# Attention and early expert products in 64-row tiles of the TensorE array

## The chip, the cores and the metric

One core of a Trainium2 chip (trn2). The metric is the device time of one execution in microseconds (us), lower is better. The span of a profile is from the first to the last instruction, about 1.8 us less than the time of the same execution. The profiled execution for the kernel before was a separate one of 525.9 us, some 7 us longer than the timed ones (517.5 to 520.2), so losses read from its trace are a few microseconds too large. Four batches of experiments ran on four chips, and the kernel before took 517.3, 523.5, 524.3 and 524.6 us on them (medians). So kernels of different batches are compared by their ratio to the kernel before of the same batch, and never by microseconds of the clock alone.

## The reference

Attention over 8 batches of 8 heads, with 576 pooled queries (the mean of two neighbours), 1152 keys and head size 64; its output is a matrix of 4608 rows of 512. Then each row goes through the two-layer network of its expert (8 experts, 512 to 1024 to 512), given by `domain_id`.

```python
q_pool = q.reshape(B, H, S // 2, 2, D).mean(axis=3)
scores = q_pool @ k.transpose(0, 1, 3, 2) / sqrt(D)
attn = softmax(scores)
x = (attn @ v).transpose(0, 2, 1, 3).reshape(B * S // 2, H * D)
for e in range(8):
    mask = domain_id == e
    out[mask] = maximum(x[mask] @ w1[e], 0) @ w2[e]
```

## The kernel before

The unit of work is a pair of heads; there are 32. A pair is cut into 12 steps, so there are 384 steps. A step makes 432 columns of scores for each of the two heads on TensorE, in the transposed form (128 keys on the partitions), and one exp instruction on ScalarE over 128 x 864. A pair needs nine "AV" chunks of 128 keys: ten products each, with the exp tile as weights and 65 columns of v (64 and a column of ones, which gives the sum of the softmax).

The head size is 64, and a product spans up to 128 rows of the array (`128*128` in the timeline). The two heads of a pair lie on rows 0 to 63 and 64 to 127, and q is kept in two copies, `qz`, with zeros in the other head's half. The scores of one head are thus a product over all 128 rows, half of them zero.

```python
def score(t):                               # one step
    p, s_ = divmod(t, SPP)                  # SPP = 12
    s = spsum.tile([P, 2, 512], FP32, name="s")
    ...
    for r in range(2):                      # the two heads
        nc.tensor.matmul(
            s[:, r, o : o + n], lhsT=kq[p][:, c * P : (c + 1) * P],
            rhs=qz[p % 2][r][:, q0 : q0 + n], start=True, stop=True)

def av(p, c):                               # one chunk of 128 keys
    for h in range(2):
        for i in range(NQ):                 # NQ = 5
            nc.tensor.matmul(
                acc[p][h][:, i * (D + 1) : (i + 1) * (D + 1)],
                lhsT=e_[:, h, o + QO[i] : o + QO[i] + P],
                rhs=v16[p % NV][:, c, h, 0 : D + 1],
                start=c == 0 and i == 0, stop=c == NC - 1, skip_group_check=True)

AVS = {3: 0, 4: 1, 5: 2, 7: 3, 8: 4, 9: 5, 11: 6, 12: 7, 13: 8}   # step: chunk
```

k and q of the next pair are transposed on TensorE against the identity (`burst_k`, `burst_q`), all in 128-row products, or 96-row ones for q (`QP = 96`). The finished rows are scattered to `x_slot` in HBM, sorted by expert; before that, `x_slot` is filled with a pattern (`init_x`, four transfers) and some rows of padding are scattered. From step 220 on, eight tiles of 128 rows of the expert work are done between the attention steps ("early tiles"); 32 tiles remain for a tail after the last exp.

The softmax here doesn't subtract the row's maximum and nothing guards it: scores larger than these inputs give would overflow.

## Time and profile before

The kernel before took 517.7 us (median of 3; with a fourth run, beside the changed kernel, 518.7 us, 517.5 to 520.2).

| what | value | where it is read |
|---|---|---|
| exp instructions, distance where nothing waits | 0.783 us | timeline of ScalarE |
| first and last exp start | 11.7 and 372.3 us | timeline of ScalarE |
| 383 x 0.783 us | 299.9 us | |
| loss of the exp chain | 372.3 - 11.7 - 299.9 = 60.7 us | worked out |
| after the last exp starts | 524.1 - 372.3 = 151.8 us | 32 expert tiles, 3.84 us each, and the ending |

ScalarE's chain of exps sets the pace up to 372 us (it is busy 78.9 of the 80 us from 140 to 220 us), TensorE sets it after that (busy 99.8 of the 100 us from 400 to 500 us). "Loss" in this document is always the time by which a stretch of exps is longer than 0.783 us each.

The first parts of the page of the kernel before: span, busy time by engine, then 40 slices of the span with the busy share in tenths, the granted TensorE clock and the busy share of the DMA engines.

```profile
span 524.1 us, 12917 instructions
...
PE 453.3 (86%) x5536; PEld 321.4 (61%) x5536; DVE 234.3 (45%) x561; ACT 348.1 (66%) x455; POOL 172.2 (33%) x294
...
PE   6679890599999999969999899999679999999990
...
ACT  2579890499999999949999899999412323323220
...
PEclk9698996699999999979999999999989999999997
...
q8 instruction: 45, 0.74, 0.6%
...
L439 ACT ACTIVATE e<-s 128x864 f16<-128x864 f32 x384 | 308.4, 895 | 59.7 <-PE s L427 56.5
```

ACT and PE are both near 9 in the attention, with a hole in the seventh and eighth slices (80 to 98 us). The last line says that ScalarE spent 59.7 us idle before exps and that almost all of it ended with a score product. The line `q8` is an instruction queue: 45 packets, 0.74 MB.

Two stretches of the timeline of the kernel before, at 98 us and from 152 us (start, duration, engine, line, operation, count, and in brackets the idle time ahead and what ended it).

```profile
98.10 0.89 ACT L439 ACTIVATE e<-s 128x864 f16<-128x864 f32 x1 [18.08 <-PE s L427]
...
152.62 0.53 PE L427 MATMUL s<-qz,kq 128*128 128x144 f16 x4
...
152.99 0.47 PE L450 MATMUL acc<-v,e 128*128 128x65 f16 x10
...
153.40 0.53 PE L427 MATMUL s<-qz,kq 128*128 128x288 f16 x4
...
153.77 0.61 PE L391 MATMUL tp<-ident,kp 128*128 128x128 f16 x8
...
154.22 0.53 PE L427 MATMUL s<-qz,kq 128*128 128x432 f16 x2
```

Durations of matmuls overlap (the scores of 152.62 last to 153.15, and AV starts at 152.99), so starts are what counts: 0.37 us from a step's scores to its AV chunk, ten AV products 29 to 35 ns apart, eight transposes 55 to 56 ns apart. The first line is the hole: one exp waits 18.08 us at step 67. There the fills of `x_slot` and the padding scatters wait for each other, and a load of q comes late behind them.

### The profile page before, as it was taken

The numbers are of one execution on the slowest core, as the hardware profiler recorded it, in microseconds if no ns is written. First come the engines' busy times: TensorE is split into PE (matmuls) and PEld (weight loads), VectorE is DVE, ScalarE is ACT, GpSimd is POOL, SyncE is SP. The second block draws the span as 40 slices with busy tenths as digits, with TensorE's granted clock in tenths as the row PEclk, the third lists the DMA queues.
The fourth block names the chain that finished last, engine by engine and source line by source line (L and its number), as shares of the span: only waits on it lengthen the run. The fifth ranks groups of instructions, "written<-read, shape, count | busy, mean of one in ns | idle before, by whom it ended". The sixth has DMA issues, their size and how long they took to land.

```text
span 524.1 us, 12917 instructions
## 1 busy us (share of the span) xinstructions
PE 453.3 (86%) x5536; PEld 321.4 (61%) x5536; DVE 234.3 (45%) x561; ACT 348.1 (66%) x455; POOL 172.2 (33%) x294
## 2 busy tenths in 40 slices
PE   6679890599999999969999899999679999999990
PEld 4457670477777777758778778777545555555540
DVE  3378640255355455525656466544323332332220
ACT  2579890499999999949999899999412323323220
POOL 5100211663613414410741633410221554312421
PEclk9698996699999999979999999999989999999997
DMA  8991547999997994994799799910051599922211
GB/s 215 240 201 22 126 135 165 250 209 236 227 231 166 192 187 72 198 216 93 171 205 208 164 153 199 203 41 34 21 176 41 125 232 269 248 93 76 86 54 44
DMA packets 53620, 81.55 MB, mean 156 GB/s; under 512 B 4783, under 2 KB 39343, under 8 KB 53553
## 3 DMA queue, kind: packets, MB, share of 16 engines
q0 software_dynamic: 35312, 50.60, 50.1%
q1 hardware_dynamic: 18032, 29.44, 21.1%
q8 instruction: 45, 0.74, 0.6%
q10 hardware_dynamic: 208, 0.59, 0.4%
q14 instruction: 23, 0.18, 0.1%
HBM read 95.48 MB, written 21.54 MB: 223 GB/s over the span
## 4 chain that ended last, share of the span: by engine, by line
PE 31%; issue 23%; DMA 18%; ACT 14%; POOL 9%; DVE 2%; POOLq 0%; SPq 0%; ACTq 0%
PE s L427 16%; ACT e L439 14%; PE acc L450 8%; POOL out_dram L349 5%; DMA x_slot<-pat 3%; DMA out_dram<-osb,xs 3%; DMA k<-in_k_dram 3%; DMA w2h<-in_moe_w_dram 2%; DMA x_slot<-pat,padr 2%; POOL x_slot L349 2%; PE m L535 2%; DMA xs<-x_slot 2%; DMA q<-in_q_dram 2%; PE m L547 2%; PE tp L391 1%
## 5 line engine op out<-in xcount | busy, mean ns | idle before, releaser
L439 ACT ACTIVATE e<-s 128x864 f16<-128x864 f32 x384 | 308.4, 895 | 59.7 <-PE s L427 56.5
L427 PE MATMUL s<-qz,kq 128*128 128x432 f16 (+2 forms) x1152 | 208.3, 290 | 12.1 <-ACT e L439 7.1
L450 PEld LDWEIGHTS <-e 128*128 128x128 f16 x2880 | 129.3, 98 | 43.4 <-issue 3.5
L450 PE MATMUL acc<-v,e 128*128 128x65 f16 x2880 | 139.1, 195 | 1.6 <-DVE xb L466 0.8
L427 PEld LDWEIGHTS <-kq 128*128 128x128 f16 x1152 | 100.2, 99 | 39.2 <-issue 18.5
L349 POOL DMA_INDIRECT out_dram<-osb,xs x40 | 40.2, 1006 | 124.4 <-ACT osb L701 65.4
L349 POOL DMA_INDIRECT x_slot<-xb,addr x40 | 42.9, 1071 | 94.3 <-issue 59.1
L678 PE MATMUL hp<-xt,w1h 128*128 128x384 f16 (+3 forms) x384 | 61.4, 311 | 1.8 <-DVE xt L664 0.9
L695 PE MATMUL op<-w2h,hT 128*128 128x512 f16 x256 | 59.8, 379 | 0.0
L678 PEld LDWEIGHTS <-w1h 128*128 128x128 f16 x384 | 34.1, 99 | 28.9 <-issue 4.6
L97 POOL DMA_DIRECT2D vs<-in_v_dram x32 | 24.2, 757 | 65.0 <-DVE v L374 52.9
L685 DVE TENSOR_SCALAR hT<-hp 128x384 f16<-128x384 f32 (+2 forms) x36 | 22.8, 632 | 49.1 <-PE hp L678 40.1
L701 ACT COPY osb<-op 128x512 f32<-128x512 f32 x20 | 11.7, 586 | 49.5 <-PE op L695 40.3
L683 ACT ACTIVATE hT<-hp 128x384 f16<-128x384 f32 (+2 forms) x36 | 19.8, 550 | 36.0 <-PE hp L678 35.6
L464 DVE RECIPROCAL rr<-acc 128x5 f32<-128x5 f32 x64 | 12.2, 190 | 70.4 <-PE acc L450 61.1
L365 DVE TENSOR_TENSOR qp<-q 96x768 f16<-96x768 f32 x32 | 30.3, 946 | 22.5 <-DMA q<-in_q_dram 22.4
L695 PEld LDWEIGHTS <-hT 128*128 128x128 f16 x256 | 24.1, 98 | 24.3
L466 DVE TENSOR_TENSOR xb<-acc,rr 128x320 f16<-128x320 f32 x64 | 31.5, 492 | 2.6
L404 PE MATMUL tp<-ident,qp 96*128 96x96 f16 x192 | 14.0, 210 | 18.1 <-DVE qp L365 18.1
L412 DVE COPY qz<-tp 64x576 f16<-64x576 f16 x64 | 28.8, 450 | 0.8
L383 DVE COPY kp<-k 128x576 f16<-128x576 f16 x62 | 25.0, 444 | 7.5 <-DMA k<-in_k_dram 7.5
L391 PE MATMUL tp<-ident,kp 128*128 128x128 f16 x256 | 20.0, 222 | 6.9 <-DVE kp L383 6.4
(93 smaller groups left out, 305.2 us busy)
## 6 DMA issues: line engine op xcount, KB each, us to landing
q<-in_q_dram SPq DMA_DIRECT2D x31, 576.0 KB, 10.1
vs<-in_v_dram POOLq DMA_DIRECT2D x32, 288.0 KB
k<-in_k_dram POOLq DMA_DIRECT2D x31, 288.0 KB
w1h<-in_moe_w_dram POOLq DMA_DIRECT2D x16, 512.0 KB
w2h<-in_moe_w_dram POOLq DMA_DIRECT2D x16, 512.0 KB
x_slot<-pat SPq DMA_DIRECT2D x4, 1285.0 KB, 9.3
xs<-x_slot SPq DMA_DIRECT2D x5, 385.5 KB, 4.6
xs<-x_slot SPq DMA_DIRECT2D x3, 642.5 KB
```

Source lines behind the costliest of these rows:

```text
L97: nc.gpsimd.dma_start(vs[:, :, :, :], v[b, h : h + 2].rearrange("h (p c) d -> p h c d", p=P))
L349: ins = nc.gpsimd.indirect_dma_start(out=dst[:, :], out_offset=bass.IndirectOffsetOnAxis(ap=ap, axis=0), in_=src, in_offset=None, **kw,)
L365: nc.vector.tensor_tensor(out=qp[:, :, :, :].rearrange("p j h d -> p h j d"), in0=q2[:, :, :, 0:D], in1=q2[:, :, :, D : 2 * D], op=ALU.add,)
L383: nc.vector.tensor_copy(kp[:, :, hh, :], loaded[p]["k16"][:, hh, :, :])
L391: nc.tensor.transpose(mt[:, c * P : (c + 1) * P], in_=kp[:, c, :, :].rearrange("p h d -> p (h d)"), identity=ident16[:, :],)
L412: nc.vector.tensor_copy(qz[p % 2][r][lo : lo + 64, :], mt[lo : lo + 64, P : P + Sp])
L427: nc.tensor.matmul(s[:, r, o : o + n], lhsT=kq[p][:, c * P : (c + 1) * P], rhs=qz[p % 2][r][:, q0 : q0 + n], start=True, stop=True,)
L439: nc.scalar.activation(e_[:, :, o : o + W], st.pop(t)[:, :, 0:W], AF.Exp, bias=0.0, scale=0.0625)
L450: nc.tensor.matmul(acc[p][h][:, i * (D + 1) : (i + 1) * (D + 1)], lhsT=e_[:, h, o + QO[i] : o + QO[i] + P], rhs=v16[p % NV][:, c, h, 0 : D ...
L466: nc.vector.tensor_tensor(out=xb[b][:, :, hh * D : (hh + 1) * D], in0=a[:, :, 0:D], in1=rr[:, :].unsqueeze(2).broadcast_to([P, NQ, D]), op ...
L678: nc.tensor.matmul(hp_[:, lo : lo + n], lhsT=w1h[:, cc, f * P : (f + 1) * P], rhs=xt[:, cc, lo : lo + n], start=cc == 0, stop=cc == ND - 1,)
L695: nc.tensor.matmul(op_[:, :], lhsT=hT[:, f, i * P : (i + 1) * P], rhs=w2h[:, f, :], start=f == 0, stop=f == NF - 1,)
```

## The change

The intent is to get TensorE time back by using the array as two independent tiles of 64 rows. One head's 64 rows of q and k are one tile, so the zero half goes. To avoid switching between tile heights, AV and the early expert products are cut into 64-row halves as well, and so are the transposes. The two halves of one product would add into the same PSUM bank at the same time. The change avoids that. So AV for three chunks is done in two crossed phases: in phase 0 the upper rows work on head 0's bank and the lower rows on head 1's, in phase 1 they are exchanged. A tiny VectorE copy, the fence, stands between two phases. All spare PSUM goes into two banks shared by transposes and expert products.

The change also makes the four fills of `x_slot` earlier (steps 18 to 26) and puts all padding scatters after them (from step 46), prepares q and k a pair earlier, loads the first expert weights every 30 steps instead of every 60 and those of three experts twice, and places early expert work by a budget of TensorE time per step.

```diff
-                    s[:, r, o : o + n], lhsT=kq[p][:, c * P : (c + 1) * P],
-                    rhs=qz[p % 2][r][:, q0 : q0 + n], start=True, stop=True,
+                    s[:, r, o : o + n],
+                    lhsT=kq[p][lo : lo + 64, c, :, :].rearrange("p a k -> p (a k)"),
+                    rhs=qt[p][lo : lo + 64, :, :].rearrange("p j n -> p (j n)")[:, q0 : q0 + n],
+                    start=True, stop=True,
...
-    def av(p, c):
+    def av(p, j, y):
...
+        for cc in range(3):
+            c = 3 * j + cc
+            for i in range(NQ) if y == 0 else range(NQ - 1, -1, -1):
+                for r in range(2):
+                    h = r ^ y
+                    lo = 64 * r
+                    nc.tensor.matmul(
+                        a[:, h, i * (D + 1) : (i + 1) * (D + 1)],
+                        lhsT=e_[lo : lo + 64, h, o + QO[i] : o + QO[i] + P],
+                        rhs=v16[p % NV][lo : lo + 64, c, h, 0 : D + 1], ...)
+        if not (j == 2 and y == 1):
+            fence(a[0:1, :, i * (D + 1) : i * (D + 1) + 1])
...
+    def turn_qk(p):
+        ...                                  # k: 9 x 2 transposes of 64 rows
+        for j in range(NJ):                  # q: 6 x (one of 64 rows, one of 32)
+            for r, n in ((0, 64), (1, QP - 64)):
+                lo = 64 * r
+                nc.tensor.transpose(
+                    mt[:, r, o + j * n : o + (j + 1) * n],
+                    in_=qp[lo : lo + n, j, :, :].rearrange("p h d -> p (h d)"),
+                    identity=ident16[lo : lo + n, lo : lo + n])
...
+    AVS = {6: (0, 0), 8: (0, 1), 10: (1, 0), 12: (1, 1), 13: (2, 0), 15: (2, 1)}
...
-        if t in (34, 37, 40, 43):
-            init_x((t - 34) // 3)
-        if 36 <= t < 36 + E:
+        if t in (18, 20, 22, 26):
+            init_x((18, 20, 22, 26).index(t))
+        if 46 <= t < 46 + E:
```

## The prediction

> **What bounds the kernel now.** The exp instructions on ScalarE follow each other every 0.783 us where nothing stalls (timeline: four in 3.13 us), so 384 of them need 300.6 us. They take 361 us: the first starts at 11.7 us, the last at 372.3 us (timeline of ScalarE). The 60 us lost: about 14 in the first 36 steps (waits for k), 20 at step 67 (ScalarE idle 18.1 us; the chain of waits shows x_slot fills and pad scatters waiting for each other at 53 to 85 us, then a q load of 10.4 us), 8 at step 219 (xs lands late), about 12 in the expert phase (0.85 per 12 steps). TensorE is nearly as full: 19.2 to 19.5 of 20 us busy in the windows from 140 to 220 us. A step needs 864 score columns, about 370 ns, and ten 65-column products, 28 ns apart, in three steps of four (timeline). After that 32 expert tiles run from 388 to 511 us, 3.84 us each, TensorE 100% busy (windows); 13 us of ending follow.
>
> **What changes.**
> 1. Scores lose the zero padding: two 64-row products should run side by side, 370 to about 190 ns a step. [...] no row tile runs in this trace, so that is an assumption.
> 2. AV becomes twice as many products of half depth. Side by side they cost 15 x 28 = 420 ns per phase, six phases a pair: 2.5 us, as now. No gain: it avoids changing the tiling[...]. Weight loads double too[...].
> 3. TensorE gets about 170 ns a step back: room for early expert work. By the kernel's own bookkeeping 13 tiles fit instead of 8, so 27 remain for the tail: 5 x 3.84 = 19 us less.
> 4. The four x_slot fills now all precede the pad scatters: the 20 us stall should go. q and k are prepared a pair ahead.
> 5. Added: fences on VectorE (estimate 0.17 us each, from the 0.19 us reciprocal), two-bank evacuations, three expert weights loaded twice. VectorE should be near 90% in the expert phase (estimate: 5.2 us per 9.4 us pair, plus 3.4 us for each of 13 tiles), so TensorE will wait for it at times. DMA was already at 1.1 shares in windows at 100 to 160 us, and weights now come twice as fast.
>
> **Sum.** 12 + 301 = 313 us without stalls; I allow 18: 8 at the start, 4 where the first xs arrives (only two steps of lead now), 6 in the expert phase. Then about 15 us until the tail's products run, 27 x 3.84 = 104, 13 of ending: 463 us profiled; unprofiled is 1.2% shorter (517.7 against 524.1): 458 us. Range 438 to 486. Chances: faster 0.95, same 0.03, slower 0.02.
>
> **What would show it.** Groups: pairs of score products start a few ns apart; an AV phase takes about 0.45 us. ScalarE: exps at 0.783 us up to step 214, no 18 us gap; last exp near 330 us. Five tiles fewer in the tail's down group (27 x 8 products instead of 256). Expert phase: exp pitch below 0.83 us.
>
> **What would make it wrong.** Row tiles that do not overlap[...]: AV phases then reach 0.8 us, and the expert phase slips by 20 to 30 us. VectorE's queue holding fences back does the same. DMA backlog from the faster weights could stall k or xs for 10 us. On the good side, if all overlaps, 440 us.

That products of two row tiles overlap was an assumption, "28 ns" is 29 ns in the median of the trace, and from 160 to 180 us TensorE was busy 18.6 us, not 19.2 to 19.5.

## The result, and the profile after

The changed kernel is slower: 564.1 us (561.8 to 568.2, 4 runs) against 518.7 us, ratio 1.088, 95% interval 1.081 to 1.096. A ratio here is the mean time of one kernel's fast runs over that of the other's of the same rounds, so it is not quite the ratio of the medians that are quoted.

The same parts of the page, for the kernel after.

```profile
span 566.4 us, 21464 instructions
...
PE 461.2 (81%) x9692; PEld 316.1 (56%) x9692; DVE 233.5 (41%) x623; ACT 348.6 (62%) x454; POOL 179.9 (32%) x306
...
PE   6767877887878877598987888889897589999993
...
ACT  2676788877898879367856767667586023232330
...
PEclk9596889979798889879888888888799699999998
...
q8 instruction: 78, 1.28, 0.9%
...
L439 ACT ACTIVATE e<-s 128x864 f16<-128x864 f32 x384 | 313.2, 907 | 116.4 <-PE s L425 114.9
...
L773 PE MATMUL op<-w2h,hT 128*128 128x512 f16 x216 | 50.8, 379 | 0.0
```

Neither engine is full in the attention any more: ACT shows 6 to 8 where it showed 9, and PE 7 to 8. ScalarE waited 114.9 us for score products (L425 is now their line). The tail's down products are 216 = 27 x 8, where the kernel before had 256; so 27 tiles remain, as the prediction said. The instruction queue has grown from 45 to 78 packets, each of 16384 bytes in the trace: the program holds 20156 instructions of TensorE, so a packet comes to about 258 of them.

The stretches of exps, from the traces. The loss is the start of the last exp less that of the first, less 0.783 us each.

```
                first exp  last exp  loss  of it in steps 0-36  36-72  72-204  204-383   after the last exp
before             11.7     372.3    60.8       11.7     23.1     3.7     22.2          151.8
after              12.8     433.7   121.0       15.1      6.1    24.0     75.8          132.7
```

The tail is 19.1 us shorter, as predicted (19), and the stall at step 67 is gone (36 to 72: 23.1 to 6.1). The whole miss lies in the chain of exps: 121 us of loss where the prediction allowed 18, and 75.8 of it come after step 204, where early expert tiles run.

The timeline of the kernel after around a set of transposes, at 148 to 152 us.

```profile
148.53 0.96 PE L425 MATMUL s<-qt,kq 64*128 64x432 f16 x4
...
149.25 0.73 PE L457 MATMUL acc<-v,e 64*128 64x65 f16 x30
...
149.80 0.44 PE L387 MATMUL m<-ident,kp 64*128 64x64 f16 x18
...
150.06 1.55 PE L396 MATMUL m<-ident,qp 64*128 64x64 f16 x12
...
151.55 0.36 PE L425 MATMUL s<-qt,kq 64*128 64x144 f16 x4
...
151.66 0.76 DVE L401 COPY kq<-m 128x1152 f16<-128x1152 f16 x1 [1.49 <-PE m L396]
...
151.95 0.89 ACT L439 ACTIVATE e<-s 128x864 f16<-128x864 f32 x1 [1.14 <-PE s L425]
```

Thirty AV products of 64 rows start within about 0.5 us, and 18 transposes of k end in 0.44 us: two 64-row tiles do work side by side. But 12 transposes of q take 1.55 us, and ScalarE loses 1.14 us to them. Their starts in the trace, with their rows:

```
150.301  64 rows
150.432  32 rows   131 ns after the one before
150.550  64 rows   118 ns
150.682  32 rows   132 ns
150.800  64 rows   118 ns
```

q is kept in groups of 96 rows. Cut at 64, it leaves a part of 32 rows, which is another tile height, and the products no longer run side by side: each starts 118 to 132 ns after the one before.

A second stretch of the same trace, ten microseconds earlier, shows a different thing.

```profile
138.79 0.61 PE L457 MATMUL acc<-v,e 64*128 64x65 f16 x29
...
140.95 0.09 PEld L457 LDWEIGHTS <-e 64*128 64x128 f16 x1 [1.68 <-issue]
...
140.96 0.20 PE L457 MATMUL acc<-v,e 64*128 64x65 f16 x1 [1.56 <-issue]
...
141.19 0.15 DVE L471 COPY fnc<-acc 1x2 f32<-1x2 f32 x1 [1.31 <-PE acc L457]
141.38 0.89 ACT L439 ACTIVATE e<-s 128x864 f16<-128x864 f32 x1 [1.50 <-PE s L425]
```

The thirtieth product of an AV phase starts 1.56 us after the end of the twenty-ninth. It waits for no semaphore; the profile calls the reason "issue", that is, none that it sees. To find it, I counted TensorE's instructions in program order and put their numbers beside the starts. In the kernel after, 21 gaps over 0.2 us have no semaphore, 23.0 us together; 12 of them lie at a number that is 192 modulo 256, and the others at 180 to 190, all after 250 us, where the count has drifted by a few. The kernel before has no such gap. The places repeat every 256 instructions, and a packet of the instruction queue comes to about 258, so I count 256 for a packet (the program is then 78.7 of them, and 78 came). And I take it that TensorE ran out of instructions; e3, e11 and e12 test that.

### The profile page after: what moved, and what is told of

It is laid out like the page before. It is cut to its first block, busy times and chain, and to the rows that moved or that the text cites. A ratio compares the mean times of both kernels' runs of the same rounds, so it can differ in the third digit from the quotient of the medians.

```text
span 566.4 us, 21464 instructions
## 1 busy us (share of the span) xinstructions
PE 461.2 (81%) x9692; PEld 316.1 (56%) x9692; DVE 233.5 (41%) x623; ACT 348.6 (62%) x454; POOL 179.9 (32%) x306
## 5 line engine op out<-in xcount | busy, mean ns | idle before, releaser
L439 ACT ACTIVATE e<-s 128x864 f16<-128x864 f32 x384 | 313.2, 907 | 116.4 <-PE s L425 114.9
L425 PE MATMUL s<-qt,kq 64*128 64x432 f16 (+2 forms) x1152 | 151.9, 317 | 40.7 <-ACT e L439 34.3
L457 PE MATMUL acc<-v,e 64*128 64x65 f16 x5760 | 139.0, 200 | 14.8 <-issue 11.4
L457 PEld LDWEIGHTS <-e 64*128 64x128 f16 x5760 | 131.2, 101 | 31.1 <-issue 22.8
L425 PEld LDWEIGHTS <-kq 64*128 64x128 f16 x1152 | 61.0, 101 | 87.2 <-issue 74.1
L756 PE MATMUL hp<-xt,w1h 128*128 128x384 f16 (+2 forms) x320 | 55.4, 317 | 2.3 <-DVE xt L742 1.5
L396 PE MATMUL m<-ident,qp 64*128 64x64 f16 (+1 forms) x384 | 51.1, 194 | 4.4 <-issue 2.6
L96 POOL DMA_DIRECT2D vs<-in_v_dram x32 | 23.9, 747 | 83.7 <-DVE v L370 65.0
L396 PEld LDWEIGHTS <-qp 64*128 64x128 f16 (+1 forms) x384 | 35.7, 93 | 17.5 <-issue 2.8
L565 PE MATMUL m<-xt,w1h 64*128 64x128 f16 x832 | 37.1, 239 | 7.7 <-DVE h L576 3.5
L565 PEld LDWEIGHTS <-w1h 64*128 64x128 f16 x832 | 32.4, 106 | 13.1 <-issue 11.9
L590 PE MATMUL m<-w2h,h 64*128 64x512 f16 x208 | 37.5, 460 | 2.2 <-DVE h L576 0.9
## 6 DMA issues: line engine op xcount, KB each, us to landing
w1h<-in_moe_w_dram POOLq DMA_DIRECT2D x22, 512.0 KB, 10.9
```

The source lines that it names most:

```text
L96: nc.gpsimd.dma_start(vs[:, :, :, :], v[b, h : h + 2].rearrange("h (p c) d -> p h c d", p=P))
L396: nc.tensor.transpose(mt[:, r, o + j * n : o + (j + 1) * n], in_=qp[lo : lo + n, j, :, :].rearrange("p h d -> p (h d)"), identity=ident16[ ...
L425: nc.tensor.matmul(s[:, r, o : o + n], lhsT=kq[p][lo : lo + 64, c, :, :].rearrange("p a k -> p (a k)"), rhs=qt[p][lo : lo + 64, :, :].rear ...
L439: nc.scalar.activation(e_[:, :, o : o + W], st.pop(t)[:, :, 0:W], AF.Exp, bias=0.0, scale=0.0625)
L457: nc.tensor.matmul(a[:, h, i * (D + 1) : (i + 1) * (D + 1)], lhsT=e_[lo : lo + 64, h, o + QO[i] : o + QO[i] + P], rhs=v16[p % NV][lo : lo ...
L565: nc.tensor.matmul(m[:, g, f * P : (f + 1) * P], lhsT=wts[e][0][lo : lo + 64, cc, (f + 4 * g) * P : (f + 4 * g + 1) * P], rhs=h0["xt"][lo ...
```

## The experiments

Thirteen kernels ran; all gave correct results. e1 to e4 shared one chip, e5 to e8 a second, e9 to e11 a third, e12 and e13 a fourth. The letters in the expectations are working names for theories, explained where they stand. The two that matter: **mixed tile heights**, and **instruction fetch** (F, later F2). Their rivals are spread through the runs: that row tiles are too slow by themselves, that early expert work, weight loads, or bursts of AV are the cause.

The loss of the exp chain in all of them, from the profiled runs (us):

```
                    first   0-36   36-72  72-204  204-383   sum  last exp
before               11.7   11.7    23.1     3.7     22.2   60.8    372.3
after                12.8   15.1     6.1    24.0     75.8  121.0    433.7
e1_q_grouped         12.1   13.0     4.2    19.2     57.4   93.8    405.8
e2_q_64              12.7   12.5     4.1    19.6     55.2   91.3    403.9
e3_no_early          12.0   13.6     2.2    23.6     12.7   52.2    364.0
e4_before_s64        12.4   11.2    21.6    -0.1     17.2   49.8    362.1
e5_spread            11.6   11.3    17.2    23.7     74.1  126.3    437.8
e6_before_fill       12.8   12.0    10.7     2.3     18.6   43.5    356.2
e7_spread_no_early   12.1   11.5    16.1    23.8     16.5   67.9    379.9
e8_fill_s64          11.9   12.2    11.5     2.1     19.5   45.2    357.0
e9_late_weights      11.3   13.0    14.3    18.9     27.1   73.2    384.5
e10_av_groups        12.4   15.1    15.5    21.3     28.9   80.7    393.0
e11_split_scores     12.4   13.1    18.1    19.9     46.0   97.1    409.4
e12_av128            11.5   10.5    13.4    11.6     13.6   49.1    360.5
e13_all128           11.6   10.2    13.2    10.8     62.2   96.5    408.0
```

### e1: the q transposes in order of their height

```diff
-        for j in range(NJ):
-            for r, n in ((0, 64), (1, QP - 64)):
+        for r, n in ((0, 64), (1, QP - 64)):
+            for j in range(NJ):
```

> The changed kernel with one loop swapped: the twelve q transposes of a pair run as six 64-row ones, then six 32-row ones, instead of alternating. Theory A (each change of tile height between consecutive products costs about 120 ns; the alternating q transposes take 1.55 us a pair for that reason): the q transposes take 0.5 to 0.7 us instead of 1.55, about 0.9 us less TensorE time in each of 32 pairs, and the kernel gets 25 to 40 us faster (about 525 to 540 us). Rival B (the loss comes from something else: instruction fetches, the clock, VectorE): the q transposes may shrink, but the time stays within 10 us of 564. Rival C (transposes of few rows are slow in themselves): the q transposes still take 1.5 us.

Measured: 543.4 us (540.3 and 546.4), ratio to before 1.049 (1.038 to 1.059). The same twelve products, only in another order, now take 0.58 us:

```profile
142.01 0.44 PE L387 MATMUL m<-ident,kp 64*128 64x64 f16 x18
...
142.28 0.58 PE L396 MATMUL m<-ident,qp 64*128 64x64 f16 x12
```

### e2: q padded to 128 rows, so that all transposes have 64 rows

```diff
+    qpb = [perm.tile([P, NJ, 2, D], F16, name=f"qpb_{i}") for i in range(2)]
+    for i in range(2):
+        nc.vector.memset(qpb[i][QP:P, :, :, :], 0.0)
...
-            for r, n in ((0, 64), (1, QP - 64)):
-                    in_=qp[lo : lo + n, j, :, :]..., identity=ident16[lo : lo + n, lo : lo + n],
+            for r in range(2):
+                    in_=qp[lo : lo + 64, j, :, :]..., identity=ident16[lo : lo + 64, lo : lo + 64],
```

> The changed kernel with q padded by zero rows from 96 to 128 partitions, so that all transposes are 64-row tiles and no product of the attention phase has another tile height. Theory A: the twelve q transposes take about 0.2 us[...], 1.35 us less a pair; [...]40 to 60 us faster than the changed kernel: 505 to 525 us. Theory A alone does not say that it beats the kernel before (518). Rival B (instruction fetches, VectorE waits in the expert phase dominate): 545 to 564 us.

(32 pairs at 1.35 us are 43 us; what the forecast of 40 to 60 us had above that was for the clock, and was not shown.)

Measured: 540.3 us (538.0 to 542.4, 4 runs), ratio 1.043 (1.036 to 1.050). The twelve transposes take 0.36 us.

```profile
142.39 0.36 PE L399 MATMUL m<-ident,qpb 64*128 64x64 f16 x12
```

What follows from both: the alternation of heights cost about 4% of the time (the ratio falls from 1.088 to 1.049 and 1.043), with nothing but the order of twelve products changed in e1. That is shown. But e2 is still 4% slower than the kernel before. And mending the transposes uncovered the other cause: gaps without a semaphore at the place 176 to 199 of 256 rose from 11 with 7.8 us to 17 with 24.3 us before step 204 (after that from 10 with 15.2 to 13 with 19.5). As I read it, a TensorE that waits for its tiles gives the fetch time, and a faster one runs into it. So the two causes don't simply add.

A gap of this kind in e2, inside one AV phase of 30 products:

```profile
155.37 0.37 PE L460 MATMUL acc<-v,e 64*128 64x65 f16 x13
...
156.38 0.44 PE L460 MATMUL acc<-v,e 64*128 64x65 f16 x17 [0.65 <-issue]
...
157.10 1.67 ACT L442 ACTIVATE e<-s 128x864 f16<-128x864 f32 x2 [0.40 <-PE s L428]
```

### e3: e2 without early expert tiles

```diff
-            elif cur is None and t >= ready and blocks and t >= 214:
+            elif cur is None and t >= ready and blocks and t >= 9999:
...
-            loads.pop(0)()
+            blocks.clear()
```

> e2_q_64 without any early expert tile: all 40 tiles run in the tail. It separates the attention phase from the expert work. If 64-row attention by itself fits under the exps, exps come every 0.783 us from step 36 to the end (excess under 0.5 us per 12 steps), the last exp ends near 325 us, and the tail takes 40 x 3.84 = 154 us: about 500 us in all. If instruction fetches or the fences hold attention up by themselves, the excess stays at 1 to 2 us per 12 steps over all 32 pairs and the last exp is after 350 us.

Measured: 552.8 us in one run (its state is unknown), 1.068 of the kernel before's median. The exps end at 364.0 us instead of 403.9, but 40 tiles stay for the tail instead of 27. So early tiles cost some 40 us of attention and are still worth doing: 13 x 3.84 = 50 us saved. The loss in steps 72 to 204, where no early tile runs in either kernel, is 23.6 us (e2: 19.6). So the slowness in the attention up to step 204 is not due to early expert work. After step 204 it is: the loss there is 12.7 us without early tiles and 55.2 with them (e2).

With less in the way, the fetch is plain here. All 26 gaps without a semaphore (34.8 us) lie at 192 modulo 256. Below are some block boundaries of e3 and of the kernel before: TensorE's gap there, and when the queue of instructions had started its last fetch.

```
e3: number  time us  gap us  last fetch started    before: number  time us  gap us  last fetch started
    3008     85.88    1.27   2.38 us earlier               2240     119.84   0.03    5.82 us earlier
    3264     91.80    0.29   2.22                          2496     128.43   0.03    6.19
    3520     97.99    2.49   2.36                          2752     138.04   0.06    7.17
    3776    104.39    0.03   2.87                          3008     146.72   0.12    5.53
    4032    109.84    1.38   2.46                          3264     155.36   0.03    6.09
    4544    119.73    0.44   3.07                          3520     163.98   0.18    5.69
    5056    133.49    4.13   2.60
```

The widest of these gaps, in the timeline of e3:

```profile
133.49 0.10 PEld L460 LDWEIGHTS <-e 64*128 64x128 f16 x1 [4.06 <-issue]
...
133.49 0.23 PE L460 MATMUL acc<-v,e 64*128 64x65 f16 x1 [3.94 <-issue]
...
134.12 1.67 ACT L442 ACTIVATE e<-s 128x864 f16<-128x864 f32 x2 [4.08 <-PE s L428]
```

In the kernel before, the fetch has started more than 5 us ahead and nothing waits. In e3, TensorE goes on 2.2 to 2.6 us after the fetch started at most of the places where it had to wait (3.1 us at one). A pair of heads needs 282 instructions of TensorE in the kernel before and 492 in the 64-row kernels, in 12 x 0.783 = 9.4 us: 256 instructions last 8.5 us and 4.9 us. A fetch does not start as soon as TensorE has crossed a boundary. In e3 it starts 2.6 us after that in the median (0.6 to 4.4 us in nine of ten), and in the kernel before 2.5 us. In e3 that and the 2.2 to 2.6 us that follow make about 5 us, as long as 256 instructions last there; in the kernel before some 6 us remain after the start. This is worked out from the two traces; what sets the start was not tested. A crossing costs TensorE up to 4 us here (4.13 us at number 5056).

### e4: the kernel before with unpadded scores alone

```diff
-                    s[:, r, o : o + n], lhsT=kq[p][:, c * P : (c + 1) * P],
-                    rhs=qz[p % 2][r][:, q0 : q0 + n], start=True, stop=True,
+                    s[:, r, o : o + n],
+                    lhsT=kq[p][64 * r : 64 * r + 64, c * P : (c + 1) * P],
+                    rhs=qz[p % 2][r][64 * r : 64 * r + 64, q0 : q0 + n], start=True, stop=True,
```

> The kernel before with the unpadded 64-row score products alone; everything else stays 128-row. Each AV chunk then has a change of tile height before and after it. Theory A: each change costs about 120 ns, so a step with an AV chunk needs 190 + 280 + 240 = 710 ns of TensorE instead of 650; steps without AV need 190 instead of 370. Net about no change: within 3% of the kernel before. If changes of height were nearly free, the score's 180 ns a step would be gained and the expert phase (0.85 us lost per 12 steps) would run at the pace of the exps: 8 to 12 us faster.

Measured: 516.0 us (515.5 and 516.4), ratio 0.996 (0.988 to 1.004): the same. It has two changes of height around each AV chunk, which the change meant to avoid. They are seen as short waits (0.18 us of the weight loads ahead of a chunk), and ScalarE doesn't notice them:

```profile
152.11 0.36 PEld L451 LDWEIGHTS <-e 128*128 128x128 f16 x10 [0.18 <-issue]
152.12 0.48 PE L451 MATMUL acc<-v,e 128*128 128x65 f16 x10
...
152.60 0.36 PE L427 MATMUL s<-qz,kq 64*128 64x288 f16 x4
```

A step is 0.78 us from scores to scores as before, and the loss in steps 72 to 204 is -0.1 us. So 64-row scores among 128-row AV chunks harm nothing, and gain nothing by themselves, for the chain of exps is the limit there.

### e5 and e7: the AV phases spread out

If the fetch only failed in bursts, the phases should be spread. e5 is e2 with AV phases every second step (the last two of six move by one step) and the transposes later; its budget then placed 12 early tiles, not 13. e7 is e5 without early tiles.

```diff
-AVS = {6: (0, 0), 8: (0, 1), 10: (1, 0), 12: (1, 1), 13: (2, 0), 15: (2, 1)}
+AVS = {6: (0, 0), 8: (0, 1), 10: (1, 0), 12: (1, 1), 14: (2, 0), 16: (2, 1)}
...
-            if cur is None and t >= ready and tq and tq[0] <= p + 1 and t not in (20, 21):
+            if cur is None and t >= ready and tq and tq[0] <= p + 1 and s_ >= 5 and t not in (20, 21):
```

> e2_q_64 with the same instructions in another order: AV phases in steps 6, 8, 10, 12, 14, 16 of a pair instead of 6, 8, 10, 12, 13, 15, and the q and k transposes in step 5 or later, where no AV phase is near, instead of step 0 between two phases. Theory F (TensorE runs out of instructions where more than 256 are used up faster than the next 16 KB fetch arrives, about 2.6 us after its start): the bursts are gone, so the 30 gaps without a semaphore wait, 44 us in e2_q_64, fall to under 10, and the kernel gets 20 to 40 us faster than e2_q_64 (500 to 520 us). Rival G (64-row tiles, fences or the clock hold TensorE up): the gaps stay, or the time stays within 8 us of 540.

> e5_spread without early expert tiles, to be read against e3_no_early (last exp at 364 us): attention alone. Theory F: no gap without a semaphore wait of over 0.2 us after step 36, exps every 0.783 us, last exp at 320 to 330 us. Rival G: last exp after 345 us.

Measured: e5 580.6 us (577.6 to 585.3), ratio 1.114 (1.105 to 1.122); e7 569.8 us (one run, state unknown), 1.089 of before. Both are slower than e2 and e3 by their ratios, and the gaps without a semaphore did not go: 44 with 47.4 us in e5 (24 of them at the boundary), 32 with 29.2 us in e7. As far as so small a spread can tell, the theory of bursts falls. What is left of it is the mean rate: spreading does not change how many instructions a pair needs.

### e6: the kernel before with the new order of the fills

```diff
-        if t in (34, 37, 40, 43):
-            init_x((t - 34) // 3)
-        if 36 <= t < 36 + E:
-            scatter(x_dram, pat[:, :], padr[:, t - 36 : t - 35], "xscat")
+        if t in (18, 20, 22, 26):
+            init_x((18, 20, 22, 26).index(t))
+        if 46 <= t < 46 + E:
+            scatter(x_dram, pat[:, :], padr[:, t - 46 : t - 45], "xscat")
```

> The kernel before with nothing but the changed order of the x_slot fills: four fills at steps 18 to 26, pad scatters from step 46, instead of in turn at steps 34 to 44. If the 19.6 us lost at steps 60 to 72 come from fills and pad scatters waiting for each other, most of it returns: 500 to 506 us. If it is plain DMA load, the loss moves elsewhere and the time stays within 5 us of 517.

Measured: 512.2 us (510.2 to 513.0) against 523.5, ratio 0.980 (0.975 to 0.986). The loss in steps 36 to 72 falls from 23.1 to 10.7 us. So this part of the change does what the prediction said, about 11 us instead of 20, for some other stalls come in its place. (The trace with 23.1 us is from another chip.)

### e8: the fills and the unpadded scores together

The edits of e4 and e6.

> The kernel before with two parts of the change alone: the order of the x_slot fills and the unpadded 64-row scores; AV, transposes and experts stay 128-row. Sum of e4 (no gain, no loss) and e6: 498 to 505 us, faster than both kernels. If the changes of tile height cost something that e4's q stall hid, it is slower than e6_before_fill by 5 us or more.

Measured: 510.3 us (508.1 to 511.7, 4 runs), ratio 0.976 (0.970 to 0.982). It is faster than both kernels, and the best: the change's two parts that need no further instruction. The interval reaches across 2%, so whether it is over 2% faster is unclear; that it is faster is not. Against e6 it gains nothing that these runs could tell (0.976 and 0.980, overlapping intervals).

### e9: e3 with its weights loaded late

A rival says that the early weight loads crowd the DMA. e9 is e3 with the five weights from step 252 on, every 12 steps, instead of from step 60, every 30.

```diff
-        if t >= 60 and t % 30 == 0 and (t - 60) // 30 < 5:
-            want_weights((t - 60) // 30)
+        if t >= 252 and t % 12 == 0 and (t - 252) // 12 < 5:
+            want_weights((t - 252) // 12)
```

> e3_no_early (all-64-row attention, no early experts) with the five expert weights loaded from step 252 on instead of from step 60, so that up to about 215 us only q, k, v and the x rows move. Theory F2 (spreading did not help, so not bursts: the next 256 TensorE instructions arrive late because their fetch queues behind the data transfers, while 64-row tiles use 256 instructions up in about 5 us instead of 8.7): the gaps at the 256-instruction boundaries before 215 us, about 30 us in e3_no_early, fall below 10 us, and step 204 starts by 190 us instead of 201 us or more. Rival H (the gaps belong to 64-row tiles and their order, whatever the DMA does): they stay above 20 us.

Measured: 573.8 us (one run, state unknown), 1.094 of before. Up to step 204 the gaps at 176 to 199 of 256 fall from 17 with 23.9 us (e3) to 8 with 6.3 us; after it, with the weights, there are 8 with 12.3 us (e3: 9 with 10.9). That fits fetches that queue behind data, but it does not show it: e9 reaches step 204 later than e3 (217.2 and 211.2 us), and a slower TensorE may have fewer late fetches anyway (before step 204, 11 such gaps in the kernel after and 17 in the faster e2). The time did not fall: other losses came, of which one is described under "What stays open". As a remedy it fails.

### e10: e8 with AV in three groups of three chunks

This tests bursts of AV without more instructions. The transposes and the early expert units move to other steps, too.

```diff
-    AVS = {3: 0, 4: 1, 5: 2, 7: 3, 8: 4, 9: 5, 11: 6, 12: 7, 13: 8}
+    AVS = {6: 0, 10: 1, 14: 2}
...
-                    c = AVS[s_ + off]
-                    av(p0, c)
-                    if c == NC - 1:
+                    j = AVS[s_ + off]
+                    for c in (3 * j, 3 * j + 1, 3 * j + 2):
+                        av(p0, c)
+                    if j == 2:
```

> e8_fill_s64 with the nine AV chunks of a pair in three groups of three, and the transposes and early expert units beside other 128-row work: fewer changes of tile height (6 instead of 18 for AV in a pair). Saves about 12 x 0.12 us = 1.4 us of TensorE time a pair. In the first half nothing is gained, since exps already come every 0.783 us; in the expert phase the excess of 0.7 us per 12 steps should fall to 0.2: 5 to 8 us faster than e8_fill_s64, 502 to 505 us. If changes of height cost nothing there, no difference.

Measured: 546.5 us (546.0 to 547.6), ratio 1.041 (1.036 to 1.046), with no gap without a semaphore at all. ScalarE is late by 0.32 to 0.33 us (median) in the step after each of the three groups, and not in the others. In its timeline, 30 products of 128 rows and the change of height after them take 1.02 us (173.81 to the scores at 174.83), and a step's scores take 0.29 us in e8, together 1.31 us against 0.783 us from exp to exp. That this is more than one step and the buffered one hold is my reading. The lateness is about half of the 21.3 us lost in steps 72 to 204 (three times 0.32 us in 11 pairs, by estimate 10.6 us); the other half comes with three stalls of 2.6 to 3.4 us of the kind described under "What stays open". So bursts that are too long cost too, without any fetch gap. This run forbids saying that everything slow here is the fetch.

### e11: e8 with every score product cut into four

The reverse: the same columns, the same AV, but 498 instructions of TensorE per pair instead of 282.

```diff
-                nc.tensor.matmul(s[:, r, o : o + n], ...)        # for r in range(2)
+            m = n // 4
+            for x in range(0, n, m):
+                for r in range(2):
+                    nc.tensor.matmul(
+                        s[:, r, o + x : o + x + m], ...
+                        rhs=qz[p % 2][r][64 * r : 64 * r + 64, q0 + x : q0 + x + m], ...)
```

> e8_fill_s64 (no gaps at 256-instruction boundaries) with each score product cut into four of a quarter of the columns: the same columns, 498 instead of 282 TensorE instructions a pair, as many as in the changed kernel; nothing else changes. Theory F2: gaps of 0.3 to 2.5 us at the 256-instruction boundaries appear, 15 to 35 us in sum, while the DMA is loaded, and the kernel gets 10 to 30 us slower than e8_fill_s64. Rival H (the gaps come with the row tiles and fences of the changed kernel, not with the number of instructions): no such gaps, at most 5 us slower.

Measured: 563.3 us (559.2 to 563.6), ratio 1.071 (1.064 to 1.077). There are 44 gaps without a semaphore, 36.7 us; 19 of them lie at 192 modulo 256. This is one, within a step's scores (timeline of e11), and below it the line of the instruction queue on its page:

```profile
162.85 0.19 PE L429 MATMUL s<-qz,kq 64*128 64x36 f16 x1 [1.35 <-issue]
```

```profile
q8 instruction: 72, 1.18, 0.9%
```

So more instructions, without crossed phases, fences or 64-row expert tiles, bring the gaps at the boundary, about 29 us of them. They are not the whole slowdown. The loss is 51.9 us above that of e8, of which some 15 us fall on the stall described under "What stays open", which e8 does not have. And the cut is not quite free on the array: from a step's first score product to the product after its scores it is 0.30 or 0.34 us, where e8 needs 0.29 us (medians between 130 and 200 us).

### e12: e3 with AV in 128-row products, in the same six phases

After eleven runs it was open how much of the 64-row kernels' loss is the number of instructions, and how much is their schedule of phases. e12 keeps the schedule, the columns and the weights of e3. Each phase does one head with 15 products of 128 rows, instead of two heads' halves with 30 of 64 rows; the fences go. TensorE's instructions fall from 18564 to 12804, or 312 per pair.

```diff
-                for r in range(2):
-                    h = r ^ y
-                    lo = 64 * r
-                    nc.tensor.matmul(
-                        a[:, h, i * (D + 1) : (i + 1) * (D + 1)],
-                        lhsT=e_[lo : lo + 64, h, o + QO[i] : o + QO[i] + P], ...)
-        if not (j == 2 and y == 1): ... fence(...)
+                nc.tensor.matmul(
+                    a[:, y, i * (D + 1) : (i + 1) * (D + 1)],
+                    lhsT=e_[:, y, o + QO[i] : o + QO[i] + P],
+                    rhs=v16[p % NV][:, c, y, 0 : D + 1], ...)
```

> This is the run without early expert tiles (e3), its weights as early and its schedule of six AV phases as they were, but each AV phase is now 15 products of all 128 rows for one head in place of 30 products of 64 rows for two. The columns that TensorE streams are the same[...], its instructions per pair fall from 492 to 312 (18564 to 12804 in all), and the fences go. Added: two changes of the tile height around each phase, about 0.12 us each by the q transposes of the first run. Theory F2 (the turnaround of the instruction fetch against the mean rate of instructions): the gaps without a semaphore at index 192 of 256 go from 26 gaps with 34.8 us to fewer than 5 with under 3 us; the loss of the exp chain in steps 72 to 204 falls from 23.6 us to below 7; the time falls from 1.068 of the kernel before to 1.01 to 1.035. Rival B (the six bunched phases, the early weights and two score buffers are too tight by themselves, and e10 lost 3% with no boundary gap at all): the loss in steps 72 to 204 stays at 18 to 25 us and the ratio at 1.055 or above. If the two changes of height per phase cost ScalarE time, the median step after a phase is late by 0.05 to 0.3 us, as it was in e10.

(In the kernel before, AV products of 128 rows are 29 ns apart in the median, and 15 of them would be about 0.44 us.)

Measured: 549.6 us (548.6 to 550.3, 4 runs), ratio 1.048 (1.046 to 1.050); e3 was at 1.068 in its one run. No gap without a semaphore is left at 192 modulo 256 (all 26 of e3 lay there), and the queue brings 49 packets instead of 71. But 20 gaps with 11.3 us remain elsewhere, where I had expected fewer than 5; most belong to a stall once per batch, described under "What stays open". The loss in steps 72 to 204 falls from 23.6 to 11.6 us. I had expected below 7. Some 7 us of the rest are accounted for: the step after the transposes is late by 0.39 us in the median (0.21 in e3), about 3 us in the pairs without a stall, and there are two of those stalls, about 2 us each, which e3 does not have. So in the attention, between steps 72 and 204, taking instructions away takes the boundary gaps away. The ratio missed its expected 1.010 to 1.035, because steps 36 to 72 lost 13.4 us here against 2.2 in e3. The other kernels of the second to fourth chips lost 11 to 18 us there, too.

### e13: e2 with AV and early expert tiles in 128-row products

As e12, with the early tiles of e2, each made of 128-row products. 13252 instructions instead of 20156.

```diff
-                    for r in range(2):
-                        g = r ^ y
-                        nc.tensor.matmul(m[:, g, f * P : (f + 1) * P],
-                            lhsT=wts[e][0][lo : lo + 64, cc, ...], rhs=h0["xt"][lo : lo + 64, ...], ...)
+                    nc.tensor.matmul(m[:, y, f * P : (f + 1) * P],
+                        lhsT=wts[e][0][:, cc, ...], rhs=h0["xt"][:, cc, :], ...)
```

> As e2 (the changed kernel with q padded to 64-row transposes), but the AV phases and the early expert tiles are made of 128-row products: one product in place of two, no fences, one PSUM bank to add up instead of two for the down product. TensorE's instructions fall from 20156 to 13252. 13 early tiles as in e2, 27 in the tail. Theory F2, with the semaphore waits of the expert phase also lengthened by late instructions: no gaps at index 192 (30 gaps with 43.8 us in e2), loss of the exp chain in steps 72 to 204 below 7 us (19.6 in e2), after step 204 between 12 and 30 us (55.2 in e2; TensorE itself is short of about 1 us per pair there by my sum 7.2 + 3.2 us against 9.4), time 0.93 to 0.985 of the kernel before, which would beat both kernels and e8. Rival B: loss after step 204 stays above 45 us and the time at or above 1.02 of the kernel before.

Measured: 541.4 us (538.9 to 542.7), ratio 1.031 (1.027 to 1.034). That is slower than the kernel before, and far from the expected 0.93 to 0.985. No gap without a semaphore lies at 192 modulo 256 in it either, and the loss in steps 72 to 204 is 10.8 us as in e12, but after step 204 it is 62.2 us (e2: 55.2). The waits of e13 between 230 and 390 us name one that has grown, of the up products for VectorE (6.3 us in 14 waits; in e2, 1.4 us in 2). The number after the total is how many waits there were, and the last is the longest:

```profile
ACT e L442 <- PE s L428: 32.8, 56, 2.2
...
PE m L552 <- DVE h L559: 6.3, 14, 0.9
```

The edit has costs of its own that I left out of the expectation: each piece of expert work of 128 rows lies between 64-row scores, with two changes of height around it, and I evacuated the up product in halves of a bank that TensorE was about to write. So e13 does not say how much of the loss after step 204 is fetch in e2. But it does say that the loss there stays without any boundary gap: e13 is e12 with 13 early tiles, and they bring it from 13.6 to 62.2 us. So a 128-row version of this schedule is no remedy.

## Why the prediction was wrong, point by point

- **What bounds the kernel, and the tail: right.** 27 tiles are left, and the part after the last exp is 19.1 us shorter.
- **"The 20 us stall should go": right** for the changed kernel; alone it is worth 11 us (e6).
- **"Side by side they cost 15 x 28 = 420 ns per phase": right in kind.** The products of one tile follow each other after 29 ns in the median, and the other tile's product starts within that time. A phase takes about 0.45 us where nothing waits. "Row tiles that do not overlap", the named danger, was not it.
- **"It avoids changing the tiling": wrong for the transposes of q.** The prediction gave this as the reason for cutting AV and overlooked that 96 rows cut at 64 leave 32. Twelve products about 120 ns apart per pair are 1.55 us instead of 0.36 us. This cost 4% (e1, e2). The sizes stood in the diff: `(0, 64), (1, QP - 64)` with `QP = 96`.
- **"No gain", the sentence on AV's cost: the first step that failed.** It counted the array's time and the weight loads, and not the instructions. A pair went from 282 to 492 of them in 9.4 us. The fetch of the next 256 then no longer hides: TensorE has boundary gaps of 24.3 us before step 204 and 19.5 us after it in e2, none in the kernel before. (Not every gap reaches ScalarE.) e11 brings the gaps by cutting products, e12 takes them away by joining them. What they are worth in time is less sure: without them the ratio falls only from 1.068 to 1.048 (e3 to e12) and from 1.043 to 1.031 (e2 to e13), with other chips, stalls and changes of height in both steps.
- **"Room for early expert work", with 6 us allowed for the expert phase: the second step that failed, and the larger miss.** After step 204 the loss is 75.8 us, and 55.2 in e2. Thirteen early tiles make it rise by 42.5 us from e3 to e2 and by 48.6 from e12 to e13, that is by 3.3 to 3.7 us a tile, nearly the 3.84 us that a tile takes in the tail. The prediction took the room from 170 ns a step and from the kernel's own bookkeeping. Since e13 has no boundary gap, the fetch alone is not the cause. Nor does the profile show TensorE full: between 240 and 380 us it is busy 95% of the time in the kernel before, 79% in e2 and 86% in e13. What costs the time between these products stays open.
- **"I allow 18" of stalls: 121 measured.** In e2, with the transposes mended, it is 91.3: 12.5 in the start (8 allowed), 23.7 in steps 36 to 204 (none allowed beyond the start), 55.2 after step 204 (10 allowed). In the last stretch, 19.5 us are boundary gaps by the count above. What TensorE's order and its waits for VectorE over the two shared banks make up of the rest was not separated; e13 was to do it and did not.
- **"VectorE should be near 90% in the expert phase": wrong.** It was busy 101.5 of the 216 us from step 204 to the last exp (47%), 41% overall. A fence took 146 ns (170 estimated). VectorE does hold TensorE up at single places (from step 204 to the last exp, 3.1 us in 6 waits for the fence and 2.9 us in 6 for `xt`), but not by its load.
- **A smaller part: the clock.** TensorE was granted half its clock in 22 spells, 96 us together, between 40 and 430 us; before it was 3 spells and 27 us, the longest of them, 17.1 us from 83.3 us on, over the hole at step 67. In e12, e3 and e2 it was 7, 12 and 13 spells, with 11.3, 34.8 and 43.8 us of gaps without a semaphore. Whether waits bring the spells, and what these cost, was not tested.

**What stays open.** The loss of the expert phase is the first thing. The second is a stall: in e5, e7 and e9 to e13, but not in e2, e3, e8 and the kernel before, TensorE, VectorE and ScalarE all slow down for 2 to 4 us about once every 48 steps, while GpSimd sends the last of five scatters to `x_slot`. This is one in e12:

```profile
122.92 0.96 POOL L348 DMA_INDIRECT x_slot<-xb,addr  x1 [0.22 <-issue]
123.60 0.28 PE L457 MATMUL acc<-v,e 128*128 128x65 f16 x4 [0.46 <-issue]
...
124.48 0.76 DVE L404 COPY kq<-m 128x1152 f16<-128x1152 f16 x1 [7.51 <-remote]
124.54 1.67 ACT L442 ACTIVATE e<-s 128x864 f16<-128x864 f32 x2 [1.95 <-remote]
```

TensorE's products come four at a time there, about 0.74 us apart, and the copy at 124.48 waited for transposes that had started by 122.01. The place is not at a block of 256. The same scatters run in e8 without any of this. I have no cause for it. It is some 2 to 4 us per batch, and with the chips' different start (steps 36 to 72) it is the larger part of why e5, e7 and e9 came out worse than the kernels that they were derived from. The chip alone does not decide it: e5 and e7 have it, and e6 and e8 on the same chip do not.

## What to carry to other kernels

Count an engine's instructions before cutting products up: halves that run side by side cost no array time (30 of them in about 0.45 us, where 15 whole ones at 29 ns would take about the same), but here 492 instructions in 9.4 us outran the fetch that 282 had left hidden, and the profile shows it only as "issue" gaps that recur every 256 instructions. When a kernel is put into one tile height, look for the remainder that makes another, for alternating heights cost about 120 ns a product, and grouping them costs an order of loops. Work that is moved under another engine's chain is not free until it is measured: 13 early tiles cost that chain 42.5 us to save 50. And change the parts one by one: the two that need no more instructions, unpadded scores and the earlier fills, took 0.976 of the time before together, nearly all of it by the fills (0.980), where the whole change took 1.088.
